# An RWKV-7 recurrence and a SiLU layer on one core: VectorE copies the inverted blocks alone, and turns the state behind odd chunks

## The chip, the core and the metric

The kernel runs on one core of a Trainium2 chip. A core has a matrix engine (TensorE, PE in the profile; its weight loads are listed apart as PEld), a vector engine (VectorE, DVE), an engine for activations and copies (ScalarE, ACT), a general one (GpSimd, POOL), and SyncE (SP), which here does nothing but issue transfers. Each engine works through its own list of instructions in order and waits for the others by semaphores. The metric is the device time of one execution, in microseconds (us).

## The reference, cut to what matters

For every batch and head, a state of 40 x 40 numbers is carried over 768 time steps; what is read from it goes, after a change of layout, through two matrix products with a SiLU between them.

```python
for t in range(S):                       # B, H, S, D = 4, 8, 768, 40
    y[:, :, t] = np.einsum('bhd,bhde->bhe', rt, state)
    Sa = np.einsum('bhde,bhe->bhd', state, at)
    state_decay = state * wt[:, :, None, :] - np.einsum('bhd,bhe->bhde', Sa, bt)
    state = state_decay + np.einsum('bhd,bhe->bhde', vt, kt)
...
h = x @ w_in                             # x: 3072 x 320, w_in: 320 x 2048
g = h * (1.0 / (1.0 + np.exp(-h)))
return (g @ w_out).astype(np.float32)    # w_out: 2048 x 320
```

## The kernel before, in words

**Tiling.** Time is cut into 12 chunks of 64 steps. A unit is one chunk of one half of the batch, so each chunk has two units (m = 0 and 1) that are worked on together. Inside a chunk the steps are solved at once: the coupling of the steps is a triangular matrix of 64 x 64 for every head, and its inverse is needed. The two diagonal blocks of 32 x 32 are inverted row by row on VectorE, for two chunks at a time (128 blocks, one per partition); the off-diagonal block follows from products on TensorE.

**The inversion** (`inverse`). The blocks come by a transfer into `mi`. Each of 31 rows is a product (line 419, into `tmp`) and a sum (line 426, into `XI`), and each depends on the one before. Then `back` copies `XI`, turned, into `mi`: ScalarE takes the first half (line 435), VectorE the second (line 436). A transfer writes `mi` to DRAM (`xd`), others read it into `XT` in another layout, and `turned` (line 463) transposes it on VectorE. The last of these for an even chunk is remembered as `mark["across"]`, the last sum of the rows as `mark["row"]`. From chunk 4 on blocks of full size are inverted (`N` is 32); before that, blocks of 16 (`N` is 16) with two more merging steps. The inversions of full size are those for chunks 4 and 5, 6 and 7, 8 and 9, 10 and 11, called the first to the fourth here.

**A chunk's chain** (`chain`): `keys` (TensorE transposes, `pt`, into `kt`), `right` (`pr`, from the state `GV`), `solve` (`pu`, `pw`, with the inverse in `XT`), `read` (`pl`, then VectorE into `vl`, line 722), `write` (`pgy`, which reads the turned state `GT` and the new keys, then VectorE updates `GV` and makes `yx`), and `turn`, which makes the turned state `GT` out of `GV` for the next chunk's `write`. `turn` has two forms: behind even chunks from 2 on, eight 32 x 32-block transposes per unit on VectorE (line 687); behind the others, 16 products with the identity per unit on TensorE and two copies on ScalarE (line 706).

**The state's tile.** `GV` holds the state in one half of the partitions and, in the other half, the values `v` of a chunk that `load_v` brings. A transpose with j = 0 and d = 1 reads 24 columns past the end of its head's range, into a part that `load_v` writes; what comes of them meets zeros.

**Scaling** (`pre`): two scans (line 335) and a reciprocal (line 336) on VectorE for each unit, and after them sums of squares on ScalarE (`junk`, lines 343 and 344). In the main loop the scaling of an even chunk is held behind `mark["row"]` for m = 0 and behind `mark["across"]` for m = 1.

**The SiLU layer** (`moe`). Its steps are a queue of filler work: `first` makes two tiles `ph` (lines 813 and 818) and ScalarE's SiLU of them, `gts` (line 820); `second` sums 16 products `po` (line 825) that read 16 such tiles. `take(n)` puts n steps in at fixed places.

**What sets the order.** The main loop (line 1025) handles chunk n (even) and n + 1 in one round, for n = 4, 6, 8, 10. TensorE's order in it is the program's, by hand. On the other engines a scheduler orders instructions by its own estimate of when they are ready and by their place in the program; `behind` and `in_order` add order without a wait. In the second half of a round the chain of the odd chunk and fillers are woven with the rows of the next inversion (line 1065), and `turn` of the odd chunk stands near the end of that. The next round opens with the first merging product of the inverse (`first`, `pq`), which needs `XT`:

```python
run(merges[1:2] + keys + merges[2:3] + right)
```

## Time and profile before

| what | value |
|---|---|
| median of 4 runs | 903.97 us (902.66 to 911.92) |
| the profiled execution | 904.08 us, of which the span of the trace is 902.3 us |
| ScalarE's half of the copy (line 435), 128 x 512 | median 1074 ns, 7 in all |
| VectorE's half of the copy (line 436), 128 x 512 | median 603 ns, longest 1564 ns, 7 in all |
| a transpose of the state on VectorE (line 687), 32 x 256 | median 435 ns, 80 in all |
| a copy of the turned state on ScalarE (line 706), 40 x 512 | median 581 ns, 24 in all |
| mean granted TensorE clock | 0.927 |

Lines of the timeline show the start and the length in us, the engine, the line of the code, the operation with its output and inputs, and how many alike were merged; in brackets stands how long the engine was idle before and who ended that. A line of a table by stretches shows, for a stretch of time, the busy time of PE, PEld, DVE, ACT and POOL with the number of instructions, then the granted TensorE clock (1.00 is full speed), the busy share of the DMA engines and GB/s. "SPq" is SyncE issuing a transfer.

### The profile page before, as it was taken

How to read it: one execution, taken by the hardware profiler on the slowest of the kernel's cores; microseconds unless marked ns; L12 is line 12 of the kernel's file. 1: busy time of each engine (PE TensorE's matmuls, PEld its weight loads, DVE VectorE, ACT ScalarE, POOL GpSimd, SP SyncE). 2: the span in 40 equal slices, each digit the busy share in tenths (PEclk: the TensorE clock that was granted, in tenths of full speed). 3: DMA queues.
4: the chain of work that ended last, by engine and by line, in shares of the span. 5: the costliest groups of instructions: out<-in, count | busy, mean ns of one | idle time of the engine just before them, and what ended most of it. 6: DMA issues, size and time to landing. Idle time of an engine off the chain costs nothing.

```text
span 902.3 us, 25358 instructions
## 1 busy us (share of the span) xinstructions
PE 778.2 (86%) x10914; PEld 551.9 (61%) x10914; DVE 561.0 (62%) x1084; ACT 297.7 (33%) x689; POOL 151.1 (17%) x156
## 2 busy tenths in 40 slices
PE   2144689895898997999998999999999989999995
PEld 2034677673776853875745857648757468574643
DVE  9979989886439598176796295992768912510000
ACT  2234457532722322614024342126150233311120
POOL 7402024200202201303012240113030000001001
PEclk9975868997769998999999999999999999999998
DMA  7875655744325542454612637315425021102001
GB/s 153 167 142 139 149 137 140 171 109 106 83 65 128 104 110 47 104 118 85 127 52 61 155 66 148 102 44 118 97 50 127 16 61 35 47 23 57 1 1 33
DMA packets 240151, 82.99 MB, mean 92 GB/s; under 512 B 207136, under 2 KB 231968, under 8 KB 240032
## 3 DMA queue, kind: packets, MB, share of 16 engines
q1 hardware_dynamic: 219488, 69.96, 35.2%
q10 hardware_dynamic: 20544, 11.34, 4.9%
q8 instruction: 87, 1.43, 0.7%
q14 instruction: 32, 0.26, 0.1%
HBM read 67.11 MB, written 14.16 MB: 90 GB/s over the span
## 4 chain that ended last, share of the span: by engine, by line
PE 51%; DVE 32%; DMA 7%; ACT 3%; SPq 3%; issue 3%; POOL 0%; POOLq 0%; ACTq 0%; DVEq 0%
PE po L825 14%; PE ph L813 10%; DVE tmp L419 9%; DVE XI L426 8%; PE pgy L264 4%; PE pl L264 4%; PE pt L264 3%; PE po L264 3%; PE ph L818 3%; PE pr L264 3%; SPq L217 3%; PE pq L264 3%; PE pm L264 2%; PE pu L264 2%; DVE w L336 2%
## 5 line engine op out<-in xcount | busy, mean ns | idle before, releaser
L825 PE MATMUL po<-wo_s,gts 128*128 128x320 f32 x768 | 223.0, 444 | 19.1 <-ACT gts L820 11.6
L825 PEld LDWEIGHTS po<-wo_s,gts 128*128 128x128 f32 x768 | 144.0, 192 | 84.1 <-ACT gts L820 16.3
L813 PE MATMUL ph<-xt,wi_s 128*128 128x512 f32 (+1 forms) x448 | 183.1, 551 | 2.6 <-ACT ot L834 1.4
L813 PEld LDWEIGHTS ph<-xt,wi_s 128*128 128x128 f32 x448 | 82.6, 194 | 83.3 <-issue 67.9
L820 ACT ACTIVATE gts<-ph 128x512 f32<-128x512 f32 (+1 forms) x112 | 54.6, 531 | 163.5 <-PE ph L818 162.8
L722 DVE TENSOR_TENSOR vl<-pl,ml 128x512 f32<-128x512 f32 x48 | 30.9, 684 | 113.9 <-PE pl L264 78.2
L419 DVE TENSOR_TENSOR tmp<-XI,mi 64x2 f32<-64x2 f32 (+40 forms) x169 | 85.6, 507 | 9.2 <-DMA mi<-md 4.1
L841 POOL TENSOR_TENSOR ot<-gts,ot 128x320 f32<-128x320 f32 x24 | 22.0, 916 | 357.9 <-ACT gts L839 352.6
L336 DVE RECIPROCAL w<-W 128x512 f32<-128x512 f32 x24 | 80.3, 3347 | 1.3
L426 DVE TENSOR_REDUCE XI<-tmp 64x2 f32<-64x2 f32 (+40 forms) x169 | 77.0, 455 | 5.2
L264 PE MATMUL pq<-XT,sb 32*32 32x32 f32 (+1 forms) x1280 | 34.8, 207 | 33.1 <-DVE XT L463 21.5
L818 PE MATMUL ph<-xt,wl_s 64*128 64x512 f32 (+1 forms) x224 | 56.9, 585 | 0.0
L264 PEld LDWEIGHTS pq<-XT,sb 32*32 32x32 f32 (+1 forms) x1280 | 31.5, 131 | 39.2 <-issue 15.8
L264 PE MATMUL pm<-a,kb 64*64 64x64 f32 x1280 | 39.5, 237 | 17.4 <-DMA kb<-in_kT 12.9
L1084 DVE TENSOR_SCALAR bad<-pb 1x1 int32<-1x1 f32 x1 | 0.1, 145 | 83.4 <-PE pb L1083 83.4
L363 POOL TENSOR_TENSOR a<-a,W 64x512 f32<-64x512 f32 x32 | 39.2, 1224 | 75.1 <-DMA a<-in_aT 52.5
L839 ACT COPY gts<-po 128x320 f32<-128x320 f32 x24 | 10.2, 426 | 122.5 <-PE po L825 94.6
L264 PEld LDWEIGHTS pm<-a,kb 64*64 64x64 f32 x1280 | 36.3, 150 | 21.7 <-POOL kb L366 15.7
L264 PE MATMUL pt<-ident,kb 128*128 128x128 f32 x192 | 30.2, 321 | 22.3 <-DVE a L308 22.3
L264 PEld LDWEIGHTS pl<-r,vut 64*128 64x128 f32 x768 | 46.0, 191 | 5.0 <-issue 2.2
L264 PE MATMUL pl<-r,vut 64*128 64x64 f32 x768 | 47.0, 276 | 2.2 <-ACT vl L650 2.0
L348 POOL TENSOR_TENSOR kb<-kb,w 128x512 f32<-128x512 f32 x20 | 24.8, 1239 | 132.2 <-DVE w L336 119.3
(108 smaller groups left out, 1065.8 us busy)
## 6 DMA issues: line engine op xcount, KB each, us to landing
kb<-in_bT SPq DMA_DIRECT2D x48, 128.0 KB
vut<-in_vT SPq DMA_DIRECT2D x48, 128.0 KB
r<-in_rT SPq DMA_DIRECT2D x24, 256.0 KB
w<-in_wT SPq DMA_DIRECT2D x45, 128.0 KB
kb<-in_kT SPq DMA_DIRECT2D x44, 128.0 KB
a<-in_aT SPq DMA_DIRECT2D x32, 128.0 KB
vl<-in_v SPq DMA_DIRECT2D x48, 80.0 KB
xs<-yx ACTq DMA_DIRECT2D x48, 80.0 KB
```

The lines of the kernel that those rows point to most:

```text
L217: x = queue.dma_start(out, in_)
L264: x = what(*x, **y)
L336: pin(nc.vector.reciprocal(R, u.W[:, :, 1 : C + 1]))
L348: nc.gpsimd.tensor_tensor(out=u.kb[:, :, 1], in0=u.kb[:, :, 1], in1=R, op=ALU.mult)
L363: nc.gpsimd.tensor_tensor(out=u.a[J, j], in0=u.a[J, j], in1=u.W[J, :, 0:C], op=ALU.mult)
L419: x = nc.vector.tensor_tensor(out=part, in0=X[L, :, t + 1 : N, t + 1 : N], in1=M[L, :, t, t + 1 : N].unsqueeze(2).to_broadcast([hi - lo, I ...
L426: x = nc.vector.tensor_reduce(out=X[L, :, t + 1 : N, t], in_=part, axis=AX.X, op=ALU.add)
L722: nc.vector.tensor_tensor(out=u.vl[:, :, j, D:], in0=pl[j].rearrange("p (q t) -> p q t", q=Q), in1=ml.unsqueeze(1).to_broadcast([128, Q, C ...
L813: in_order(nc.tensor.matmul(ph[n], lhsT=wi_s[:, k, at : at + 128], rhs=xt[:, k, :], start=k == 0, stop=False))
L818: in_order(nc.tensor.matmul(ph[n], lhsT=wl_s[R, i, :], rhs=xt[R, 2, :], start=False, stop=True))
L820: nc.scalar.activation(out=place(2 * i + n)[:, T], in_=ph[n], func=AF.Silu)
L825: in_order(nc.tensor.matmul(po[:, 0:DM], lhsT=place(f)[:, b * 128 : b * 128 + 128], rhs=wo_s[:, NF // 2 * half + f, :], start=f == 0, stop ...
```

## The change: who copies the blocks, and who turns the state

Three things are edited. In `back`, for full-size blocks, VectorE copies all 32 columns and ScalarE none; and `mark["row"]` is now this copy, so that the scaling of m = 0 stands behind it. In `turn`, the VectorE form is also taken behind the odd chunks 5, 7 and 9 (chunk 11 has no `turn`, chunks 1 and 3 keep the TensorE form). These transposes are held over: they run in the next round, after the second part of the even chunk's `solve` and before its `read`, and on VectorE not before `mark["across"]`. The number of filler steps stays; the list that is woven with the rows is two steps shorter.

```diff
         def back():
             turned = XI.rearrange("p t s -> p s t")
-            nc.scalar.copy(out=mi[L, 0:16], in_=turned[L, 0:16])
-            pin(nc.vector.tensor_copy(out=mi[L, 16:32], in_=turned[L, 16:32]))
+            at = 0
+            if N == 16:
+                at = 16
+                nc.scalar.copy(out=mi[L, 0:16], in_=turned[L, 0:16])
+            x = nc.vector.tensor_copy(out=mi[L, at:32], in_=turned[L, at:32])
+            pin(x)
+            mark["row"] = x.ins
             send(queue, xd[L], mi[L])
...
         def turn():
-            if u.n > 1 and u.n % 2 == 0:
+            if u.n > 1 and u.n != 3:
                 wide = GVf[u.m]
...
-                            nc.vector.transpose(
+                            x = nc.vector.transpose(
                                 out=gt[T, :, 32 * e : 32 * e + 32],
                                 in_=wide[E, at : at + Q * D].rearrange("p (q d) -> p q d", q=Q)[:, :, 0:32],
                             )
+                            if u.n % 2 == 1:
+                                behind(x, mark["across"])
                 return
...
+    held = []
     for n in range(4, NN, 2):
...
-        run(solve[1:2] + later[2:3] + [x[i] for i in (2, 7, 3, 8) if x] + read)
+        run(solve[1:2] + later[2:3] + [x[i] for i in (2, 7, 3, 8) if x] + held + read)
...
-        turn = start(n + 1)[5] if n + 2 < NN else []
+        held = start(n + 1)[5] if n + 2 < NN else []
...
-            x += [partial(fetch, 0), partial(queue.extend, more), partial(take, 2)] + turn
+            x += [partial(fetch, 0), partial(queue.extend, more), partial(take, 2)]
             weave(x + [partial(take, 1)] * 6, rows[1:36])
```

## The prediction

> **What bounds the kernel now.** I read the page first, then TensorE's waits after 350 us, then the timeline around each inversion's end, then the busy time by stretches.

> ```profile
> span 902.3 us, 25358 instructions
> ...
> PE 778.2 (86%) x10914; PEld 551.9 (61%) x10914; DVE 561.0 (62%) x1084; ACT 297.7 (33%) x689; POOL 151.1 (17%) x156
> ```

> By shares TensorE is the bound. The waits of TensorE from 350 us on say where it still stands idle:

> ```profile
> PE po L825 <- ACT gts L820: 9.8, 6, 3.3
> PE pq L264 <- DVE XT L463: 5.9, 4, 3.7
> ```

> Both sit at the ends of the four inversions. The timeline at the third one (chunks 8 and 9):

> ```profile
> 598.91 1.13 PE L818 MATMUL ph<-xt,wl_s 64*128 64x512 f32 x4
> 599.47 1.16 DVE L426 TENSOR_REDUCE XI<-tmp 128x31 f32<-128x961 f32 x1
> 600.54 1.28 DVE L335 TENSOR_TENSOR_SCAN W<-w,one 128x260 f32<-128x260 f32 x2
> 600.66 1.08 ACT L435 COPY mi<-XI 128x512 f32<-128x512 f32 x1 [4.62 <-DVE XI L426]
> 601.64 0.59 ACT L820 ACTIVATE gts<-ph 128x512 f32<-128x512 f32 x1
> 601.76 0.35 SPq L217 DMA_DIRECT2D xd<-mi  x1
> 601.92 3.35 DVE L336 RECIPROCAL w<-W 128x512 f32<-128x512 f32 x1
> 602.28 6.26 PE L825 MATMUL po<-wo_s,gts 128*128 128x320 f32 x16 [2.24 <-ACT gts L820]
> ...
> 606.58 0.70 DVE L463 STREAM_TRANSPOSE XT<-XT 32x512 f32<-32x512 f32 x1 [1.30 <-DMA XT<-xd]
> 607.63 0.70 DVE L463 STREAM_TRANSPOSE XT<-XT 32x512 f32<-32x512 f32 x1 [0.35 <-DMA XT<-xd]
> ...
> 608.47 1.20 PE L264 MATMUL pq<-XT,sb 32*32 32x32 f32 x64
> ```

> ScalarE stands 4.62 us before its half of the copy, as the rows aren't done. The SiLU `gts` queued behind waits too, and TensorE, which ran out of `ph` at 600.04, waits 2.24 us for it. That wait is what the change takes away. But read on: the inverse is in `XT` at 608.33 (607.63 + 0.70), and the first product that needs it starts at 608.47. Two chains end together here. The stretches show which one is tight:

> ```profile
> 484.50:544.90 60.40, 59.98 (x1141) 44.65 (x1140) 34.90 (x57) 27.62 (x66) 16.90 (x16) 1.00 0.45 96
> 557.20:600.60 43.40, 41.90 (x355) 24.84 (x353) 41.14 (x84) 6.79 (x13) 3.98 (x4) 1.00 0.32 79
> ```

> From 557.2, when the blocks land, to 600.6 VectorE has 41.14 of 43.40 us busy with a chain of rows (and the odd chunk's `write`); only short gaps between instructions are left. The round is a loop: from `pq` to the scores of the next odd chunk it is TensorE's (the first row, 59.98 of 60.40 us busy), 12.3 us of transfers bring them to `mi` (557.2), 43.4 us of rows follow, 7.8 us later `XT` is ready and the next `pq` starts. Between 545 and 608 TensorE only does fillers and short pieces of the odd chain, sized to last about as long.

> **The change, part by part.** R is the end of the rows, R' the new one.

> *Odd turns leave TensorE.* In rounds 4, 6 and 8, 64 products go; at 574.99 they take until 576.90, when the next `po` starts: 1.91 us, 5.7 us in all. They lie in the stretch that VectorE's rows bound, so TensorE only arrives earlier at the wait for `XT`: worth 0, and 5.7 us only if rows and transfers stopped being the bound. With them go 12 copies of 0.58 us on ScalarE, which was idle 3 to 4 us between SiLUs there: 0.

> *Odd turns come to VectorE.* 16 transposes x 0.435 = 7.0 us a round, behind the even chunk's transposes of `XT`. In the third round VectorE is idle from 614.4 (odd `XT`) to 631.7 (`vl`, line 722), 17.3 us: 0. A quarter of them (j = 0, d = 1) read columns that the load of the next `v` writes; SyncE issues these loads from 613.71 to 619.09. With 2.2 us to land (`XT`: issue 604.43, in use 606.58) VectorE could stand until 621.3 and still has 10 us before `vl`. Behind the standing transposes only `vl` is queued, and `GT` is read at 639. The other loads that SyncE issues there, and GpSimd's scalings, touch neither `GV` nor `GT`. Without that cover they would cost up to 7 us a round, with the load late, more.

> *The copy.* Before, VectorE's half ran early (574.78, between two rows, as those columns were done) and pushed the rows by 0.51 us (next sum at 575.29). That goes: R' = R - 0.5. At R' one copy of 1024 elements follows. No row shows it: doubling the 603 ns of 512 elements, less the start (I take 1.17 ns an element) gives 1.13 us; bounds are 0.6 (the half's time) and 3.1 (twice the longest, 1564 ns). I take 1.13, since five of the seven are of its form and near 0.6. Before, R to the transfer's issue was 1.13 us (600.63 to 601.76), so the issue is at the same place behind R': -0.5 us for each of four inversions, -2.1 us. [...]

> *The scaling of m = 0 is now behind the copy.* Scan and reciprocal end at R' + 1.13 + 1.28 + 3.35 = R' + 5.8; `XT` lands at R + 5.95 (606.58 - 600.63). It still fits, with 0.2 us to spare: 0; each us that the copy takes longer delays the transfer and this alike, and counts once. GpSimd's scaling of the keys follows 0.6 us later and is used only by the scores, tens of us on: 0.

> *ScalarE is freed.* All SiLUs run on time, TensorE goes straight on. In the third round `ph` would end at 598.1 (600.04 - 1.91), its 16 `po` take 4.57 us, and from 602.7 to 607.9 TensorE has nothing but `pq`, which waits for `XT`: 5.2 us idle in one piece. In the second the same sum gives 477.8 to 484.0. So 9.8 us of waits don't vanish; they become the wait for `XT`. And such a wait has a price. The first inversion already shows one:

> ```profile
> 357.19 0.31 PE L264 MATMUL pq<-XT,sb 32*32 32x32 f32 x2 [3.74 <-DVE XT L463]
> 358.31 1.91 PE L264 MATMUL pq<-XT,sb 32*32 32x32 f32 x62 [0.81 <-DVE XT L463]
> 360.15 3.67 PE L264 MATMUL pt<-ident,kb 128*128 128x128 f32 x16
> ```

> and in stretches of 1 us:

> ```profile
> 361.00:362.00 1.00, 1.00 (x7) 1.00 (x6) 1.00 (x1) 0.94 (x2) 0.00 (x0) 0.50 0.00 0
> ```

> The granted clock fell to 0.50 from 354 to 364 us, and the 16 `pt` took 3.67 us against 1.97 at full clock (609.61). From `pq` at 358.31 to `pr` at 365.07 it is 6.76 us; at the second inversion, at full clock, 4.26 (484.59 to 488.85): 2.5 us lost, on TensorE's own 60 us of the loop. At the fourth it is 5.68 (731.07 to 736.75): 1.4 lost. The second and third lose none on the path today: waits there are cut up by the late SiLUs (3.29 us at 475.2 left the clock at 1.00), or the slow part fell under the `po` (0.59 and 0.50 from 603 to 606.6). With 5 to 6 us in one piece I take the nearest row, the first's 2.5, for all four: +2.5 and +2.5 for second and third, +1.1 for the fourth, 0 for the first. Bounds: 0, and 3.4 (the whole stretch from resuming at half clock, 6.8 us, lost by half) each.

> [...]

> Sum on the profiled 904.08 (0.1 above the median): -2.1 + 6.1 = +4.0, so 908.

> **The rivals.** (1) *Forecast*, 0.5: as above; 904.5 to 911.
> (2) *The clock holds*, 0.2: no drop hits the new gaps; the copy's gain alone, 904.1 - 2.1 = 902, and 898 if the two losses of today (2.5 + 1.4) go too. For it: 3.29 us left the clock whole. Against: 5 us did not exist then.
> (3) *SiLUs queue behind another instruction*, 0.18, slower: the sums of squares (`junk`) wait for the reciprocal, which is now at R' + 5.8. In the second and third inversions two SiLUs stand behind them (605.31, then 605.94 and 607.03). If the scheduler keeps that order, `po` ends 3.2 us after the reciprocal (481.47 to 484.66), at R' + 9.0, past `XT` at R' + 7.8: +1.2 on two inversions and a longer slow stretch, up to +1 each: 910.5 to 913. It decides once one SiLU of the last pair stands behind `junk`. Against it: with `turn` gone TensorE is 1.9 us earlier there and the reciprocal 0.6 later, and in the first inversion, where TensorE was early, both SiLUs stand first.
> (4) *TensorE is the bound after all*, 0.07: 5.7 + 9.8 us less, 888.6. Against: 41.14 of 43.40.
> (5) A new order on VectorE that delays rows or `XT`, 0.05: above 913.

> **How the numbers follow.** The likeliest is 908. Leaving out (4), (5) and the outer ends of (2) and (3), the range is 900 to 913. About 1% (9 us) is what can be told from no change: faster by that 0.06 (case 4), slower 0.11 (5, and the upper end of 3 with a slow copy), the rest between.

> **What would show it.** Right: no ScalarE copy at the rows' end; `po` of line 825 without its wait for `gts`; `pq` waiting 4 to 6 us for `XT` in the second and third inversions, clock 0.50 after it and `pt` above 3 us; the copy near 1.13 us; transposes of line 687 after the odd `XT` with `vl` not later. Wrong: `pq` starting over 1 us sooner behind the rows' end than the 7.8 us of today, or full clock there.

## The result, and the profile after

The changed kernel takes 910.1 us in the median, beside 903.7 us for the kernel before. The ratio is 1.0056, with a 95% interval of 1.0041 to 1.0071: 3.7 to 6.4 us slower. The profiled execution took 909.11 us (span 907.3) against 904.08 us (span 902.3), so the two traces differ by 5.0 us, and they can be laid side by side.

The head of the page after (the engines' busy time, share of the span and instructions):

```profile
span 907.3 us, 25000 instructions
...
PE 777.3 (86%) x10722; PEld 553.3 (61%) x10722; DVE 582.0 (64%) x1132; ACT 287.4 (32%) x673; POOL 150.6 (17%) x156
```

192 records of TensorE and 16 copies of ScalarE have gone, 48 instructions of VectorE have come, and TensorE is busy as long as before, in spite of its 192 records less. (The profile has two records for each fp32 product of this kernel: eight products added further on leave 16. So these are 96 products, a `second` sums 8 products that read 8 tiles, not 16, and counts such as 62 `pq` or 16 `pt` are records.) That is the first hint: the products that are left take longer. The waits of TensorE from 350 us on (what waited, for whom: us in total, times, longest):

```profile
PE pq L264 <- DVE XT L468: 21.2, 8, 5.1
```

The 9.8 us of `po` waiting for `gts` are gone (no such line is left) and the 5.9 us of `pq` waiting for `XT` have become 21.2. The timeline around the third inversion's end shows how (the copy is now line 439, `gts` 828, `po` 833, the transposes of `XT` 468, those of the state 692):

```profile
596.46 4.57 PE L833 MATMUL po<-wo_s,gts 128*128 128x320 f32 x16
596.56 1.08 ACT L828 ACTIVATE gts<-ph 128x512 f32<-128x512 f32 x2 [3.54 <-PE ph L826]
...
598.26 1.06 DVE L439 COPY mi<-XI 128x1024 f32<-128x1024 f32 x1
...
604.01 0.63 ACT L343 ACTIVATE junk<-w 128x512 bf16<-128x512 f32 x1 [6.37 <-DVE w L336]
604.19 0.70 DVE L468 STREAM_TRANSPOSE XT<-XT 32x512 f32<-32x512 f32 x1 [0.21 <-DMA XT<-xd]
...
604.94 0.31 PE L264 MATMUL pq<-XT,sb 32*32 32x32 f32 x2 [3.91 <-DVE XT L468]
...
605.93 1.91 PE L264 MATMUL pq<-XT,sb 32*32 32x32 f32 x62 [0.68 <-DVE XT L468]
...
607.77 3.62 PE L264 MATMUL pt<-ident,kb 128*128 128x128 f32 x16
...
612.46 2.06 PE L264 MATMUL pr<-GV,a 128*64 128x40 f32 x64
```

Both SiLUs stand ahead of `junk`, `po` goes through without a break and ends at 601.03, and TensorE has nothing more until `pq`. The rows end at 598.23, and the 62 `pq` start 7.70 us later (7.84 before): the wait was taken off ScalarE and lies in front of `pq` now. Then comes the price. In the table by stretches (busy time of PE, PEld, DVE, ACT, POOL, then the granted clock) two stretches show it, one behind this wait and one 23 us later:

```profile
609.00:610.00 1.00, 1.00 (x7) 1.00 (x6) 1.00 (x1) 0.80 (x2) 0.00 (x0) 0.50 0.00 0
...
632.00:633.00 1.00, 1.00 (x12) 1.00 (x12) 0.81 (x2) 0.00 (x0) 0.00 (x0) 0.50 0.43 94
```

The clock is 0.50 in both. Summed over the stretches from 330 us on, TensorE worked at half clock for 13.0 us before and for 29.9 us after; if work takes twice as long there, half of the 16.9 us of difference, 8.5 us, is time that TensorE lost, on the critical path or off it. That is an estimate: the 16 `pt` took 3.62 us at half clock against 1.97 at full clock, 1.84 times as long, which would make it 7.7 us.

The loop's three full rounds, from one inversion's `pr` to the next one's, put the whole difference in its place (us, before / after):

| stage of the round | 1st | 2nd | 3rd | sum of differences |
|---|---|---|---|---|
| `pr` to the scores of the odd chunk (TensorE's) | 54.16 / 54.15 | 54.19 / 54.75 | 54.76 / 57.98 | +3.8 |
| scores to the first row (transfers) | 13.28 / 13.82 | 14.22 / 14.54 | 11.55 / 11.68 | +1.0 |
| rows (VectorE's) | 44.30 / 42.46 | 43.44 / 42.15 | 44.30 / 44.84 | -2.6 |
| end of the rows to the 62 (or 64) `pq` | 7.78 / 7.87 | 7.84 / 7.70 | 7.79 / 7.66 | -0.2 |
| `pq` to `pr` (TensorE's small tiles) | 4.19 / 5.94 | 4.20 / 6.53 | 5.68 / 6.91 | +5.3 |

That is +7.3 us. The first `pr` lies 2.5 us earlier than before (362.55 against 365.07), of which 2.1 us were there at the first row of the first inversion already, ahead of all that was changed in the order of the loop; other kernels with the same first part began that row anywhere from 306.6 to 312.8 us. What follows the last `pr` differs by 0.2 us.

### The profile page after: what moved, and what is told of

Its sections match the earlier page's. It is cut to its first block, busy times and chain, and to the rows that moved or that the text cites. A ratio compares the mean times of both kernels' runs of the same rounds, so it can differ in the third digit from the quotient of the medians.

```text
span 907.3 us, 25000 instructions
## 1 busy us (share of the span) xinstructions
PE 777.3 (86%) x10722; PEld 553.3 (61%) x10722; DVE 582.0 (64%) x1132; ACT 287.4 (32%) x673; POOL 150.6 (17%) x156
## 4 chain that ended last, share of the span: by engine, by line
PE 42%; DVE 21%; DMA 5%; SPq 2%; issue 2%; ACT 1%; POOL 0%; POOLq 0%; ACTq 0%; DVEq 0%
PE po L833 13%; PE ph L821 8%; DVE tmp L419 7%; DVE XI L426 7%; PE pgy L264 3%; PE pl L264 3%; PE ph L826 2%; PE pt L264 2%; SPq L217 2%; PE pm L264 2%; PE pq L264 2%; PE po L264 2%; PE pr L264 2%; PE pu L264 1%; DVE GV L769 1%
## 5 line engine op out<-in xcount | busy, mean ns | idle before, releaser
L336 DVE RECIPROCAL w<-W 128x512 f32<-128x512 f32 x24 | 80.2, 3342 | 1.0
L426 DVE TENSOR_REDUCE XI<-tmp 64x2 f32<-64x2 f32 (+40 forms) x169 | 76.8, 455 | 5.1
L264 PE MATMUL pq<-XT,sb 32*32 32x32 f32 (+1 forms) x1280 | 37.5, 214 | 47.6 <-DVE XT L468 36.7
L264 PEld LDWEIGHTS pq<-XT,sb 32*32 32x32 f32 (+1 forms) x1280 | 34.0, 137 | 54.1 <-DVE XT L468 28.9
L692 DVE STREAM_TRANSPOSE GT<-GV 32x256 f32<-32x256 f32 x128 | 55.7, 435 | 11.2 <-DMA GV<-in_v 9.2
L264 PE MATMUL pm<-a,kb 64*64 64x64 f32 x1280 | 40.6, 240 | 17.9 <-POOL kb L366 15.5
L264 PE MATMUL pt<-ident,kb 128*128 128x128 f32 x192 | 32.8, 340 | 23.2 <-DVE a L308 23.2
L264 PEld LDWEIGHTS pm<-a,kb 64*64 64x64 f32 x1280 | 37.2, 153 | 22.3 <-POOL kb L366 15.7
L847 ACT COPY gts<-po 128x320 f32<-128x320 f32 x24 | 10.2, 426 | 125.3 <-PE po L833 105.6
L264 PE MATMUL pl<-r,vut 64*128 64x64 f32 x768 | 47.6, 278 | 2.2 <-ACT vl L655 2.0
L264 PEld LDWEIGHTS pl<-r,vut 64*128 64x128 f32 x768 | 46.4, 193 | 4.9 <-issue 2.2
```

What stands on the lines that cost most here:

```text
L264: x = what(*x, **y)
L336: pin(nc.vector.reciprocal(R, u.W[:, :, 1 : C + 1]))
L426: x = nc.vector.tensor_reduce(out=X[L, :, t + 1 : N, t], in_=part, axis=AX.X, op=ALU.add)
L692: x = nc.vector.transpose(out=gt[T, :, 32 * e : 32 * e + 32], in_=wide[E, at : at + Q * D].rearrange("p (q d) -> p q d", q=Q)[:, :, 0:32],)
```

## The experiments

Three questions were open: which of the two parts costs, whether it is the clock, and whether the gap can be used. "Half clock" is TensorE's busy time at half clock from 330 us on, in the profiled run (13.0 before, 29.9 after); the four times are those from the 62 `pq` (64 where none came early) to `pr` at the four inversions (6.76, 4.19, 4.20, 5.68 before; 6.99, 5.94, 6.53, 6.91 after). Each ratio is to the kernel before, run beside it on the same chip.

| run | ratio, 95% interval | `pq` to `pr`, us | half clock, us |
|---|---|---|---|
| the copy alone | 1.0103 [1.0073, 1.0133] | 7.30, 7.19, 7.19, 5.74 | 40.8 |
| the turns alone | 1.0087 [1.0055, 1.0119] | 5.94, 6.33, 6.67, 6.96 | 22.3 |
| the copy alone, SiLUs first | 1.0048 [1.0019, 1.0078] | 7.30, 5.68, 5.76, 7.16 | 34.8 |
| after + 8 dense products in the gap | 0.9947 [0.9913, 0.9982] | 4.15, 6.86, 4.15, 4.36 | 6.4 |
| after + 4 dense products | 1.0012 [0.9985, 1.0040] | 6.58, 5.75, 7.23, 4.15 | 22.9 |
| after + 120 small products | 1.0081 [1.0046, 1.0117] | 5.67, 6.58, 7.23, 7.69 | 36.0 |
| after, a filler moved to the gap | 0.9790 [0.9747, 0.9833] | 4.15, 4.15, 5.76, 4.15 | 10.2 |
| before, a filler moved | 0.9910 [0.9875, 0.9945] | 4.19 in all four | 13.6 |
| copy alone, SiLUs first, filler moved | 0.9811 [0.9774, 0.9847] | 5.69, 4.19, 4.20, 4.20 | 6.8 |
| turns alone, filler moved | 0.9835 [0.9790, 0.9880] | 4.15 in all four | 13.6 |
| after, all fillers halved and spread | 1.0223 [1.0187, 1.0259] | 4.19, 4.20, 4.20, 4.15 | 0 |
| after, only `second` halved and spread | 0.9777 [0.9745, 0.9809] | 5.67, 5.74, 4.15, 4.15 | 6.8 |

### The copy alone

The kernel before, with the first part of the change (`back` and `mark["row"]`) and TensorE's turns kept:

```diff
-            nc.scalar.copy(out=mi[L, 0:16], in_=turned[L, 0:16])
-            pin(nc.vector.tensor_copy(out=mi[L, 16:32], in_=turned[L, 16:32]))
...
+            x = nc.vector.tensor_copy(out=mi[L, at:32], in_=turned[L, at:32])
+            pin(x)
+            mark["row"] = x.ins
```

> The kernel before with only the copy's part of the change: VectorE copies the whole inverted blocks, the odd turns stay on TensorE. Theory (the time goes into half-clock stretches after a gap in TensorE's work ahead of pq): the wait for gts goes, TensorE stands about 3 us in one piece for XT in the second and third inversions, and the clock drops there in most runs; pq to pr takes 5 to 7 us instead of 4.26; ratio to the kernel before 1.001 to 1.005. Rival (the held turn on VectorE is what costs): without it this is 2 us faster, ratio 0.998, pq to pr as before.

The ratio is 1.0103, more than the whole change costs; the theory had 1.001 to 1.005 and missed. The timeline at the second inversion (here `gts` is line 825, `po` line 830):

```profile
482.64 0.63 ACT L343 ACTIVATE junk<-w 128x512 bf16<-128x512 f32 x1 [9.20 <-DVE w L336]
...
483.27 1.06 ACT L825 ACTIVATE gts<-ph 128x512 f32<-128x512 f32 x2
...
483.90 1.34 PE L830 MATMUL po<-wo_s,gts 128*128 128x320 f32 x4 [3.52 <-ACT gts L825]
...
485.18 1.81 PE L264 MATMUL pq<-XT,sb 32*32 32x32 f32 x64
```

ScalarE stood 9.20 us before `junk`, which waits for the reciprocal, while the two SiLUs behind it were ready to run. `po` ends past the time at which `XT` is ready (484.48), so `pq` starts 8.32 us behind the rows' end (9.47 at the third inversion) instead of 7.7. This is the prediction's rival 3, in the kernel with the copy alone; the change itself escapes it.

### The turns alone

The changed kernel with the old `back`: ScalarE's half of the copy is put back, and `mark["row"]` is the rows' last sum again.

```diff
-            x = nc.vector.tensor_copy(out=mi[L, at:32], in_=turned[L, at:32])
-            pin(x)
-            mark["row"] = x.ins
...
+            nc.scalar.copy(out=mi[L, 0:16], in_=turned[L, 0:16])
+            pin(nc.vector.tensor_copy(out=mi[L, 16:32], in_=turned[L, 16:32]))
```

> The kernel before with only the turn's part of the change: the odd turns behind chunks 5, 7 and 9 are held over and made on VectorE, the copy stays half on ScalarE. Theory (gap and clock): TensorE comes 1.9 us earlier to a wait for gts that ends when it ended before, so that wait is 4 us long, the clock drops under the po behind it, and these end near or somewhat after XT is ready; ratio 0.999 to 1.004, vl not later. Rival (the held turn costs by itself, through its wait for the load of v or the order on VectorE): ratio 1.005 or more, with vl or the scores late against pr.

The ratio is 1.0087; the theory had 0.999 to 1.004 and missed. TensorE's waits tell why:

```profile
PE pq L264 <- DVE XT L463: 17.7, 8, 3.7
```

With 1.91 us of turns off TensorE, it reaches the inversion's end earlier, and the waits in front of `pq` grow from 5.9 to 17.7 us, though ScalarE still has its copy; all four times from `pq` to `pr` are those of a fallen clock, 5.9 to 7.0 us. The turns are not the whole of it, for the scheduler also made another order on ScalarE. The third inversion before, and with the turns alone:

```profile
605.31 0.63 ACT L343 ACTIVATE junk<-w 128x512 bf16<-128x512 f32 x1 [3.08 <-DVE w L336]
605.94 0.58 ACT L820 ACTIVATE gts<-ph 128x512 f32<-128x512 f32 x1
```

```profile
604.00 1.08 ACT L823 ACTIVATE gts<-ph 128x512 f32<-128x512 f32 x2
607.66 0.63 ACT L343 ACTIVATE junk<-w 128x512 bf16<-128x512 f32 x1 [2.58 <-DVE w L336]
```

Before, the last SiLUs stand behind `junk` and `po` ends 7.9 us behind the rows' end; here they stand ahead of it, `po` ends 3.0 us behind, and the waits for `gts` are 4.7 us in all where the theory had 4 us each. Taking work off TensorE where the rows are the bound was costed at 0; with the order that came with it, it cost the clock.

### The SiLUs put first

The copy alone, with `junk` of m = 0 held behind the last SiLU, so that only the order which cost the first run here its time is undone:

```diff
+                mark["silu"] = x.ins
...
+            if "pair" in mark and u.n % 2 == 0 and u.m == 0:
+                behind(x, mark["silu"])
```

> e1 (only the copy's part) with one order added on ScalarE and no wait: the first sums of squares of m = 0 of an even chunk stand behind the last SiLU issued. Theory (e1's 1% is the SiLUs queued behind these sums, 3.5 us twice, and the clock they lose): po of the last filler no longer waits for gts, TensorE stands 2 to 3 us for XT in the second and third inversions, and the ratio falls from e1's 1.010 to 1.000 to 1.005. Rival (the order costs nothing, something else in the copy's part does): 1.008 or more.

1.0048 instead of 1.0103. The 7.0 us in which `po` waited for `gts` are gone and `pq` waits 14.3 us for `XT` instead of 8.5. By the medians, the order of the SiLUs behind `junk` cost about 5 us of the copy's 9 (the two intervals just touch). And it shows what the turns are worth in the change: without them TensorE is 1.91 us later in that stretch, and the scheduler, which orders by its own estimate, puts `junk` first; with them it does not.

### Is it the clock? Dense products in the gap

The changed kernel with eight products of 128 x 128 x 320 ahead of the next round's `pq`. Their result is read by nobody.

```diff
+    def warm(k):
+        pd = bank("pd")
+        for f in range(k):
+            product(nc.tensor.matmul, pd[:, 0:DM], lhsT=ident, rhs=wo_s[:, f, :], start=True, stop=True)
...
+        warm(8)
         run(merges[1:2] + keys + merges[2:3] + right)
```

> The changed kernel with eight products of the identity and a weight tile, which nothing reads, put on TensorE ahead of each first pq (some 4.5 us of work at full clock, in the gap where it waits for XT). Nothing else is edited. Theory: the clock stays at 1.00 there, pq to pr takes 4.2 to 4.4 us in all four inversions against 5.9 to 7.0 in the changed kernel, and 5 to 9 us come back: ratio to the kernel before 0.995 to 0.999, to the changed one 0.99 to 0.995. Rival (the clock is not what costs): the added work gives nothing, ratio to the kernel before 1.005 or above.

More work, less time: 0.9947. The timeline at the third inversion (`pd` are the added products, two records each):

```profile
598.49 4.47 PE L264 MATMUL pd<-wo_s,ident 128*128 128x320 f32 x16
...
603.56 1.19 PE L264 MATMUL pq<-XT,sb 32*32 32x32 f32 x62 [0.43 <-DVE XT L468]
604.69 1.97 PE L264 MATMUL pt<-ident,kb 128*128 128x128 f32 x16
```

The same 62 `pq` take 1.19 us instead of 1.91, the `pt` 1.97 instead of 3.62. With the clock up, the change makes the kernel 5 us faster, as the prediction's rival 2 had it (898 to 902). At the second inversion a wait of 1.64 us and another of 0.86 remained, and the clock fell there (6.86 us).

With half as many products:

```diff
-        warm(8)
+        warm(4)
```

> As e3, with four products instead of eight (2.2 us), so that some 2 to 3 us of gap stay. Theory (what matters is the share of a stretch of about 3.4 us in which the array works, and the gap is followed by 1.2 us of small pq): the clock still drops in half or more of the inversions, ratio 0.998 to 1.004, between e3 and the changed kernel. Rival (only an idle stretch of the full 3.4 us counts): no drop, as e3, 0.993 to 0.998.

1.0012, between the two. With waits for `XT` of 1.25 to 2.44 us left, the clock fell at three of the four inversions (6.58, 5.75 and 7.23 us from `pq` to `pr`, 4.15 at the fourth), so the rival's idle stretch of 3.4 us was not needed; at the third inversion the waits were 1.71 and 0.93 us. The 3.4 us of the theory is the length in which the slow stretches come (603.18 to 606.59 us in the kernel before). That the share of work in such a stretch sets the clock was the author's estimate.

### Is it idleness, or what TensorE is busy with?

Now 120 products of 32 x 32 fill the gap instead (again read by nobody):

```diff
+                    product(
+                        nc.tensor.matmul,
+                        pd[R, h * 32 : h * 32 + 32],
+                        lhsT=ident[R, R],
+                        rhs=ident[R, R],
...
+        warm()
         run(merges[1:2] + keys + merges[2:3] + right)
```

> The changed kernel with 120 products of 32x32 tiles, which nothing reads, in the gap ahead of each first pq, instead of e3's eight of full tiles: TensorE is busy about as long (64 records of such pq take 1.2 us, so 4.5 us), with a small part of the array. Theory A (idle time on TensorE is what lets the clock drop): as e3, ratio 0.995 to 0.999, pq to pr 4.15 us. Theory B (the clock goes by how much of the array works, so small tiles count little): the clock is 0.50 at pq in most inversions although TensorE was busy, pq to pr 5.5 to 7 us, ratio 1.004 or more, as the changed kernel or above.

1.0081: they help nothing. The timeline at the second inversion, and below it the stretches of 1 us there:

```profile
471.07 3.04 PE L264 MATMUL pd<-ident 32*32 32x32 f32 x180
475.06 1.27 PE L264 MATMUL pd<-ident 32*32 32x32 f32 x60 [0.95 <-issue]
...
479.10 3.67 PE L264 MATMUL pt<-ident,kb 128*128 128x128 f32 x16
```

```profile
473.00:474.00 1.00, 1.00 (x70) 1.00 (x65) 1.00 (x1) 0.00 (x0) 0.00 (x0) 1.00 0.00 0
474.00:475.00 1.00, 0.11 (x8) 0.02 (x1) 0.98 (x1) 0.00 (x0) 0.00 (x0) 1.00 0.57 90
475.00:476.00 1.00, 0.94 (x57) 0.94 (x58) 0.56 (x1) 0.95 (x3) 0.94 (x1) 0.94 0.75 117
476.00:477.00 1.00, 0.50 (x15) 0.36 (x9) 0.64 (x2) 0.81 (x3) 1.00 (x2) 0.50 0.84 141
```

TensorE (the first share behind the stretch's length) is busy without a break from 471.07 to 474.11 and, after a pause of 0.95 us, again from 475.06; at 475.9 the clock falls. The wait in front of the 62 `pq` is down to 0.76 us and yet they are no faster. With dense products in the same place the clock stays at 1.00 at three of the four inversions. Being busy was not what kept it up: with 120 small products the clock fell at all four (5.67 to 7.69 us from `pq` to `pr`). The two kinds differ in the size of the tile, in the columns of a product (320 against 32) and in the numbers they multiply, and no run separates these. The small ones also run on a little too long: the 62 `pq` start 8.0 to 8.7 us behind the rows' end, 7.7 to 8.2 in the changed kernel.

### Using the gap

A filler (`second`, 4.57 us) that stood between `right` and `solve` of the even chunk, where TensorE is the bound, is moved to the end of the round before, ahead of `pq`. Nothing is added or left out:

```diff
-    take(8)
+    take(9)
...
         each(load, n + 3)
-        take(1)
...
-            weave(x + [partial(take, 1)] * 6, rows[1:36])
+            weave(x + [partial(take, 1)] * 7, rows[1:36])
```

> The changed kernel with one filler step a round moved: the one between right and solve of the even chunk goes, and one more stands at the end of the rows, ahead of pq (before the first round too). Theory: the gap of 4 to 5 us ahead of pq is filled by 4.6 us of work that no longer stands on TensorE's 60 us between pq and the scores, and the clock holds: 3 to 5 us a gap and 1.5 to 2.7 us of clock, four times: 885 to 893, ratio to the kernel before 0.98 to 0.988. Rival (TensorE's total work is the bound and gaps cost only themselves somewhere else): within 0.5% of the changed kernel.

0.979: 2.1% faster than the kernel before. At the second inversion:

```profile
462.48 8.88 PE L833 MATMUL po<-wo_s,gts 128*128 128x320 f32 x32
...
471.97 1.19 PE L264 MATMUL pq<-XT,sb 32*32 32x32 f32 x62 [0.43 <-DVE XT L468]
```

32 records of `po` run up to 471.36 where 16 stood, and the 62 `pq` start 7.70 us behind the rows' end, as without them, at full clock. From `pr` to the scores the first and third round take 49.7 us instead of 54.2 and 58.0. The time comes from two sides: 4.5 us of TensorE a round moved out of the stretch that it bounds, and full clock behind three of the four inversions. In the second round the clock fell at 481.5 (55.0 us to the scores). The move has a price there: `pu` now waits for `RHS`, which the filler used to cover, and small tiles follow.

```profile
479.51 1.02 PE L264 MATMUL pu<-RHS,XT 64*64 64x40 f32 x27 [1.32 <-ACT RHS L633]
```

The same diff on the kernel before, on the copy alone with the SiLUs first, and on the turns alone says what each part is worth beside it:

> The kernel before with the same filler step a round moved as in e4, and nothing of the change. Theory: TensorE has no free time ahead of pq here (it arrives with XT in the second and third inversions), so the moved 4.6 us only shift, pq starts as much later as the stretch behind it is shorter; only the first inversion has a real gap (3.7 us): ratio to the kernel before 0.990 to 1.000, and e4 stays some 1.5% faster. Rival (the moved filler is a gain by itself, the change has no part in e4's time): ratio 0.975 to 0.985, as e4.

> e7 (the copy's part, SiLUs ahead of the sums of squares) with the filler moved as in e4; the odd turns stay on TensorE. Theory (work taken off TensorE in the rows' stretch is worth its time once a filler is there to use it): TensorE is 1.9 us a round longer ahead of pq than in e4, in three rounds, so some 1.9 x 3 less the 0.5 to 0.9 us that e4 still waits: 3 to 5 us behind e4, ratio to the kernel before 0.982 to 0.986. Rival (the odd turns on VectorE give nothing even then): as e4, 0.979.

> e2 (the turn's part; the copy stays half on ScalarE) with the filler moved as in e4. Theory: the SiLUs still stand behind ScalarE's half of the copy, up to 1 or 2 us of TensorE's time a round, but the pq that follows has the moved filler in front, so 2 to 6 us behind e4: ratio 0.981 to 0.988. Rival (ScalarE's half of the copy costs nothing once the gap is filled): as e4, 0.979.

0.991, 0.981 and 0.9835; the second lies between its theory and its rival. In the kernel before, `po` waits 8.5 us for `gts` with the longer queue, and `pq` starts 8.9 to 12.2 us behind the rows' end: the filler runs past the time at which `XT` is ready. There it gains 0.9%. With the change the same move reaches 0.979, 1.2% lower than that by the medians. Either part by itself gets most of it, and the three intervals overlap; the copy alone with the filler and without the SiLUs put first was not tried.

### Finer fillers

Is what is left of the lost clock due to long runs of small tiles between the dense ones? All fillers were cut in halves and spread over the same places:

```diff
+        def first_half(T, i, n):
...
+            R = slice(64 * n, 64 * n + 64)
+            in_order(nc.tensor.matmul(ph, lhsT=wl_s[R, i, :], rhs=xt[R, 2, :], start=False, stop=True))
...
+            steps += [partial(second, half, b, part) for b in range(4) for part in range(2)]
...
-    take(9)
+    take(15)
```

> e4 with every filler of the main loop cut into two steps of half the work, and the even chunk's three fillers spread in halves over its five places, so that no stretch of small tiles between two fillers is longer than 3.7 us but the one behind pq; the same products in all. Theory (small tiles let the clock drop as e6 showed; e4 still spends 10 us of work at half clock behind 330 us): up to 5 us less than e4, ratio to the kernel before 0.973 to 0.979. Rival (the drops in e4 come from what waits remain at pq, not from the small tiles behind it): as e4 or slower, 0.979 to 0.985, with the clock dropping at the same places.

A miss: 1.0223, though the clock was 1.00 from 330 us to the end of the loop. The cut had split the pair of products of 64 rows that read the two halves of the rows of `wl_s`. The first line is from this run, where two records stand alone, the second from the next run, where four stand together (lines 823 and 826 are the same product):

```profile
455.73 1.12 PE L823 MATMUL ph<-xt,wl_s 64*128 64x512 f32 x2
```

```profile
461.36 1.13 PE L826 MATMUL ph<-xt,wl_s 64*128 64x512 f32 x4
```

Two take as long as four, so each `first` was about 1.1 us longer. In the last run only `second` was cut:

```diff
-            steps += [partial(first_half, T, NF // 4 * half + i, n) for i in range(NF // 4) for n in range(2)]
+            steps += [x for i in range(NF // 4) for x in (partial(first, T, NF // 4 * half + i), lambda: None)]
```

> The changed kernel with one filler moved ahead of the first products of the inversion's blocks, as in the best run so far (0.979), but every second cut into two halves of eight records, spread over the same places, and each first kept whole. Theory (what is left of the lost clock comes from stretches of small tiles with few dense products in them, so spreading the dense ones finer holds it): the granted clock is 1.00 behind every inversion, first to last product of the small tiles takes 4.15 to 4.3 us in all four, and the time is 0.973 to 0.979 of the kernel before. Rival (the drops that are left come from the waits at the inversion, which are not made shorter): the times behind the inversions stay as in the kernel with the moved filler or get worse, and the ratio is 0.979 to 0.985. Either way a first's four products that read wl_s should take about 1.13 us together again, which is what tells whether the cut of the firsts alone cost the 40 us of the run with both cut.

The four `wl_s` are back at 1.13 us and the ratio is 0.9777, in the theory's range but not to be told from the 0.979 of the moved filler (the intervals overlap nearly whole). The slow stretch at 481 is gone: `pr` to scores is 50.0 to 50.4 us in all three rounds. But at the first and second inversion the clock still fell behind `pq` (5.67 and 5.74 us, not the 4.15 expected), where waits of 0.4 to 0.9 us remain. Waits as long at the third and fourth left it at 1.00. So with the finer spread the clock held in the middle of the round, and not at the inversion; the cut also puts half a filler between `right` and `solve` again, so that the wait of `pu` for `RHS` is gone, and which of the two held it is not shown. It stays open how much of these last 3 us can be had.

## Why the prediction was right

The forecast was 908.0 us, with 904.5 to 911 for the likeliest case; the median is 910.1. The steps, one by one:

- **Turns off TensorE, worth 0.** They bring no time by themselves, as said. But an earlier TensorE means a longer gap, and the turns alone, with the order on ScalarE that came with them, cost 0.87%. The sum had the gap from both parts together, so its total is not hurt; the 0 for this part alone was wrong.
- **Turns on VectorE, hidden.** Right. The transposes stand for a load as named, once in two of the rounds (1.10 and 1.76 us) and twice in the last (4.60 and 1.72), and VectorE then still waits 10.4 to 10.6 us for other things before `vl`, which in the third comes at 631.52 (631.69 before):

```profile
620.04 0.88 DVE L692 STREAM_TRANSPOSE GT<-GV 32x256 f32<-32x256 f32 x2 [1.76 <-DMA GV<-in_v]
631.52 1.29 DVE L730 TENSOR_TENSOR vl<-pl,ml 128x512 f32<-128x512 f32 x2 [10.60 <-ACT XT L561]
```

- **The copy.** 1.06 us in the median of the four, against 1.13: 1.04 ns an element, against 1.18 in the half-size copy. The 1.13 was an estimate from the 603 ns of that half, and it was 0.07 us too long. Issue of the transfer and start of `pq` came as forecast. The rows were shorter by 1.84 and 1.29 us in two rounds and longer by 0.54 in the third, where 0.5 less was expected in each; with the copy alone they took 42.66, 42.91 and 44.29 us. What else moved them was not tried.
- **The reciprocal fits, by 0.2 us.** Right to the tenth: VectorE stood 0.21 us before `XT`.
- **SiLUs ahead of `junk`.** Right for the change. The copy alone shows that the order was close to going the other way, and rival 3's price there was about 5 us, the top of its bracket (910.5 to 913, 2.5 to 5 above the forecast).
- **The waits merge into one gap.** Right in kind: 5.10, 3.97, 3.91 and 4.87 us in front of `pq`, against 5.2 and 6.2 forecast for third and second, and two products that come early part it from another 0.7 to 1.1 us.
- **The clock loss.** The mis-sized term, though little so: +2.5, +2.5 and +1.1 were taken for second, third and fourth, and +1.75, +2.33 and +1.23 were measured, 5.3 for 6.1; the first lost 0.2 more where 0 stood. (The second `pr` of before starts at 488.78, not 488.85, so full clock is 4.19 us and not 4.26; the 2.5 stands.)
- **What the sum did not have.** A second slow stretch, from 631 to 638 us, where no wait of any length precedes it: TensorE is busy for 3.19 of the 3.42 us from 628.28 to 631.70. `po` at 634.63 took 6.49 us instead of 4.57, and the scores of that round came 3.2 us later. Since 626.2 TensorE had had only products of at most 64 columns, on tiles of 32 x 32 to 64 x 128:

```profile
628.00:629.00 1.00, 1.00 (x63) 0.96 (x61) 0.00 (x0) 0.94 (x4) 0.00 (x0) 1.00 0.91 212
...
630.00:631.00 1.00, 0.78 (x15) 0.64 (x13) 0.00 (x0) 0.91 (x2) 0.00 (x0) 1.00 0.80 177
```

Of the 3.8 us in the stage's row 3.2 are this; with 1.0 us in the transfers they put the three rounds 2.7 us above the forecast (+7.3 for +4.6), though rows and clock came out better. The head of the trace, 2.0 us below the forecast by luck (other kernels differ there by up to 6 us), hides most of that in the total. In the profiled run of before the same products run from 626.4 to 633.5 at full clock, and no such stretch stands in the middle of a round; in the kernel before with the moved filler one comes there too, from 622.26 to 629.08. Whether it comes each time is open: one execution of each kernel was profiled.

That it is the clock and not some other cost of the gap is shown: eight products that do nothing turn 1.0056 into 0.9947. That the slower clock comes from waiting alone, as the forecast had it, is not: 120 small products in the same gap left it as slow (1.0081).

## What to carry to other kernels

A wait that is taken off one engine is only gone if something useful stands in its place; here it moved 5 us on, became one piece, and the matrix engine came out of it at half clock. Before taking work off an engine that waits anyway, look for dense work to put into the gap: one filler moved there turned a loss of 0.6% into a gain of 2.1%, with no more work. Cut such work by whole groups: here two records that read `wl_s` took 1.12 us alone and four together 1.13, and that cut cost more than the gap had (1.0223 against 1.0056).

## What the runs showed of the hardware

**Being busy did not hold the clock.** Four stretches of 3.41 us, the length of the shortest slow ones, that start whole multiples of it from the slow stretches of their run: two in a row from the kernel before, one from the changed kernel, one from the kernel with 120 small products:

```profile
473.47:476.88 3.41, 1.70 (x6) 0.30 (x4) 3.34 (x4) 0.04 (x1) 0.00 (x0) 1.00 0.00 0
476.88:480.30 3.42, 1.84 (x7) 1.36 (x8) 3.32 (x3) 1.53 (x2) 0.00 (x0) 1.00 0.38 153
```

```profile
600.97:604.38 3.41, 0.06 (x1) 0.00 (x0) 3.20 (x2) 0.37 (x1) 0.33 (x1) 1.00 0.46 109
```

```profile
472.47:475.88 3.41, 2.46 (x157) 2.37 (x151) 2.96 (x2) 0.83 (x3) 0.82 (x1) 1.00 0.39 64
```

Busy for 50% and 54% with dense products, TensorE kept its clock. Busy for 0.06 us, it fell to 0.50 at the stretch's end; and busy for 72% with products of 32 x 32, it fell as well. Nor did being busy bring it back: behind the third inversion of that run it stayed at 0.50 for 13.7 us, TensorE busy in nearly all of them, until `po` had run for 3.5 us, while in the changed kernel it was back at 611.22, behind 3.4 us of `pt`. What small products do to the clock beyond this is open.
